# Moving the weight sums between gaps, and the order of three turns on VectorE, in a linear-attention and mixture kernel

## The chip, the cores and the metric

The kernel runs on one core of a Trainium2 chip. The metric is the device time of one execution in microseconds (us), lower being better; for the kernel before it is the median of three runs. All data are 32-bit floats.

## What is computed

Two blocks are chained. The first is a linear recurrence over time (4 batches, 8 heads, 768 steps, head width 40): each head holds a 40 x 40 state.

```
for t in range(S):
    y[t]  = r[t] @ state
    Sa    = state @ a[t]
    state = state * w[t] - outer(Sa, b[t]) + outer(v[t], k[t])
```

Its output is laid out as 3072 tokens of 320 features, `x`. The second block is a mixture of four experts with hidden width 1024:

```
p   = domain_probs / (sum(domain_probs) + 1e-9)
out = sum over e of  p[:, e] * (relu(x @ w1[e]) @ w2[e])
```

## The kernel before

**Units and passes.** The sequence is cut in chunks of 64 steps, and the batches in pairs, so there are 24 units of 64 steps of two batches and all heads. The text counts them from 0: unit 3 is the fourth. Inside a chunk the recurrence becomes small matrix products and a triangular solve. A loop (`for u in range(1, NU)`) makes one pass for each unit. In pass `u` three units are in work at once: unit `u` finishes (its last products with the state and its features `xT`), unit `u+1` has its solve merged and its state products begun, and unit `u+2` goes through `within` and starts its solve. The third pass of the change's title is that of unit 2 and the fifth that of unit 4, if the work ahead of the loop is counted as unit 0's.

**`within` (L402)** prepares a unit. On VectorE it turns W by 32 x 32 blocks (`turn_raw`, L239), scans it to a decay G (L439), takes a reciprocal (L451), makes the tiles `n_tok` (L471) and `k_tok` (L476), turns A (`AT`, L478) and multiplies it by G (L480), and turns V and R (`VT`, `RT`, in `turn_rv`, L421). TensorE then makes the scores `pc` from RT and VT (`causal_scores`, L463), and `pfe` from AT and the turned `n_tok` and `k_tok`. The turns all stand under line 241 in the profile.

**`substitute` (L542)** is the triangular solve of a unit. VectorE and ScalarE copy `blocks` out of `F`, VectorE turns them to `M` (L553) and does two steps (L565, L569), and then GpSimd (POOL in the profile) runs some 48 small operations on `Z` (L580, L593), in a chain. **`merge` (L599)** turns the result back on VectorE (`Qc` L604, `QTc` L606); TensorE makes `pY` from QTc, ScalarE copies `Yq`, TensorE makes `pQ`, ScalarE copies `QT` (L627).

**`step` (L636)** joins a unit to the state: `prn` on TensorE; `RH` on VectorE (L654) and `SN` on ScalarE (L659), both out of `prn`; then `psat` on TensorE, which needs RH and QT; then `pxr`, `pdy`, the state's update and the features.

**The mixture** is work for TensorE that fills the waits of all this. It stands in a list `todo` of pieces: `ups` makes hidden activations (`ph`, relu on ScalarE to `hs`), `down` multiplies them by w2 (`po`, `p`) and VectorE adds the product, scaled by the gate, to the output tile `osb` (L789, L791). The products `ph`, `po`, `p` share three slots of PSUM (tag "mm", `bufs=3`). For the first two units (one chunk) the product with w2 is plain. From the second chunk on, two units are done together by Strassen's scheme with seven products for eight: it needs sums of activations (`add_h`, L897) and **sums of blocks of w2** (`add_weights`, L863): five VectorE operations of 128 x 640 elements for each of four experts, 20 in all, made once. Three of the five are written to a tile `sums`, two over parts of w2 itself, so an expert's sums may come only after its plain products of the first chunk.

**What sets the order.** Each pass has four gaps. `gap(n)` first runs as many weight sums as `sums_at` says for its number `4 * u + n`, then one or two pieces of `todo`. A scheduler at build time lays out each engine's queue; an instruction that is marked with `keep_in_program_order` keeps its place in the program on its engine, the others go where the scheduler finds them ready. [...] All matmuls are marked up to pass 5 (`EARLY`), the weight sums, `Qc`, `QTc`, `blocks`, `M` and the first solve steps always. In `within` the helper `pin` (L406) marks an instruction only for units 0 to 3 (`PADDED` is 3); the turns of V and R are not marked at all.

**In pass 2 to 4** the program runs, in this order: gap 0; the scan's use and `n_tok`, `k_tok` and the turns of unit `u+2`; gap 1; the rest of unit `u`'s step; the products `pc` and `pfe` of unit `u+2`; the merge of unit `u+1` and the solve of unit `u+2`; gap 2; W's turn and the scan of unit `u+3`; `RH` of unit `u+1`; gap 3; `psat` of unit `u+1`.

## Time and profile before

| | |
|---|---|
| median of three runs | 1103.84 us (1103.26 to 1104.54) |
| the profiled execution | 1102.3 us, its span 1100.6 us |
| TensorE busy | 1070.0 us (97% of the span) |
| VectorE busy | 756.6 us (69%) |
| ScalarE busy | 353.0 us (32%) |
| GpSimd busy | 502.9 us (46%) |
| the 20 weight sums on VectorE | 12 of 845 ns and 8 of 872 ns, from 138.2 to 252.5 us |
| granted TensorE clock, mean | 0.991 |

The span is the time between the first and the last recorded instruction; the execution's own time has 1.7 us more around it, and lies 1.5 us under the median of the runs. PE is TensorE's matmuls, PEld its weight loads, DVE is VectorE, ACT ScalarE, POOL GpSimd, and SPq the queue that issues most DMAs. "L863" is line 863 of the kernel. A wait is listed with the instruction that waited and, after the arrow, the one whose end released it, as far as the profile can tell; "issue" means that the profile names no releaser.

### The profile page before, as it was taken

The page shows a single profiled execution, that of the slowest core. Times are in us where ns is not written, and L with a number is a line of the kernel's source. Part 1 is how long each engine was busy: PE and PEld are TensorE (multiplying, and loading weights), DVE is VectorE, ACT ScalarE, POOL GpSimd, SP SyncE. Part 2 cuts the span into 40 slices and gives each one's busy share as a digit, 9 for nine tenths or more (in the row PEclk, how much of TensorE's full clock was granted, in tenths as well). Part 3 has the DMA queues.
Part 4 walks back from the last instruction along what each step waited for, and adds up shares of the span by engine and source line. Part 5 has one row for each costly group of instructions (what it writes and reads, how often), then busy time and mean ns, then how long its engine had stood idle before and what let it go on. Part 6 is the DMA issues. An engine that isn't in the chain of part 4 may idle for free.

```text
span 1100.6 us, 38528 instructions
## 1 busy us (share of the span) xinstructions
PE 1070.0 (97%) x16102; PEld 955.8 (87%) x16102; DVE 756.6 (69%) x1551; ACT 353.0 (32%) x956; POOL 502.9 (46%) x1274
## 2 busy tenths in 40 slices
PE   6799899999999999999999999999999999999998
PEld 6677788789998999898999989989998989988887
DVE  7766668887777776767767768767767677543343
ACT  2432444223233233243233242332332432321110
POOL 5106677753463653743734635636537437430000
PEclk9799999999999999999999999999999999999999
DMA  7776545425345363354353444443552532222320
GB/s 117 226 247 138 136 103 117 119 55 136 98 111 127 98 140 97 94 146 103 93 144 94 102 121 104 116 120 84 127 123 65 147 85 67 98 69 82 104 76 13
DMA packets 268868, 122.18 MB, mean 111 GB/s; under 512 B 213736, under 2 KB 242072, under 8 KB 268696
## 3 DMA queue, kind: packets, MB, share of 16 engines
q1 hardware_dynamic: 265416, 119.12, 43.0%
q8 instruction: 127, 2.08, 0.8%
q10 hardware_dynamic: 3280, 0.61, 0.3%
q14 instruction: 45, 0.37, 0.1%
HBM read 111.79 MB, written 3.93 MB: 105 GB/s over the span
## 4 chain that ended last, share of the span: by engine, by line
PE 81%; DVE 7%; POOL 5%; ACT 3%; issue 2%; DMA 1%; SPq 0%; ACTq 0%; DVEq 0%; POOLq 0%
PE ph L76 35%; PE p L76 28%; POOL Z L593 3%; PE pdy L76 3%; PE psat L76 2%; PE pxr L76 2%; POOL Z L580 2%; PE prn L76 1%; PE pfe L76 1%; PE pQ L76 1%; PE po L76 1%; PE pc L76 1%; DVE Z L590 1%; PE pY L76 1%; DVE M L553 1%
## 5 line engine op out<-in xcount | busy, mean ns | idle before, releaser
L76 PE MATMUL ph<-xT,w1p 128*128 128x256 f32 (+3 forms) x3040 | 446.3, 377 | 4.0 <-issue 3.9
L76 PEld LDWEIGHTS ph<-xT,w1p 64*64 64x64 f32 (+1 forms) x3040 | 338.5, 162 | 72.7 <-issue 29.0
L593 POOL TENSOR_TENSOR Z<-Z 128x31 f32<-128x31 f32 (+7 forms) x704 | 260.0, 369 | 55.2
L897 DVE TENSOR_TENSOR a<-hs 128x512 f32<-128x512 f32 x220 | 151.8, 707 | 104.7 <-ACT hs L778 104.7
L580 POOL TENSOR_TENSOR Z<-M,Z 128x62 f32<-128x62 f32 (+7 forms) x352 | 144.1, 409 | 132.3 <-DVE M L569 106.4
L778 ACT ACTIVATE hs<-ph 128x512 f32<-128x512 f32 (+1 forms) x208 | 115.3, 564 | 226.5 <-PE ph L76 225.4
L76 PE MATMUL p<-sums,a 128*128 128x160 f32 x1056 | 164.9, 299 | 0.0
L76 PEld LDWEIGHTS p<-sums,a 128*128 128x128 f32 x1056 | 152.8, 190 | 2.2
L791 DVE SCALAR_TENSOR_TENSOR osb<-p,gate,osb 128x320 f32<-128x320 f32 (+1 forms) x243 | 108.1, 481 | 57.8 <-PE p L76 53.6
L550 POOL COPY below<-F 32x256 f32<-32x256 f32 x48 | 22.8, 475 | 198.7 <-ACT F L506 197.0
L76 PE MATMUL p<-w,a 128*128 128x160 f32 x704 | 105.9, 301 | 0.2 <-ACT hs L778 0.2
L76 PE MATMUL p<-w,hs 128*128 128x160 f32 x704 | 102.9, 299 | 0.0
L76 PEld LDWEIGHTS p<-w,hs 128*128 128x128 f32 x704 | 100.2, 190 | 2.2
L76 PEld LDWEIGHTS p<-w,a 128*128 128x128 f32 x704 | 98.3, 190 | 3.0 <-ACT hs L778 3.0
L612 POOL COPY QT<-QTc 32x256 f32<-32x256 f32 x96 | 51.7, 539 | 76.9 <-DVE QTc L606 67.7
L553 DVE STREAM_TRANSPOSE M<-blocks 128x1024 f32<-128x1024 f32 x24 | 47.4, 1977 | 38.1 <-ACT blocks L547 37.9
L700 ACT COPY RS<-pxr 64x256 f32<-64x256 f32 x88 | 32.2, 366 | 105.2 <-DVE SX L400 43.1
L451 DVE RECIPROCAL gp<-gp 128x320 f32<-128x320 f32 x24 | 51.6, 2151 | 0.7
L535 ACT COPY EV<-pev 64x160 f32<-64x160 f32 x96 | 23.1, 286 | 89.7 <-PE pev L76 89.3
L604 DVE STREAM_TRANSPOSE Qc<-Z 128x256 f32<-128x256 f32 x24 | 15.0, 627 | 46.2 <-POOL Z L593 46.1
L627 ACT COPY QT<-pQ 32x128 f32<-32x128 f32 x96 | 24.6, 256 | 59.9 <-PE pQ L76 58.2
L659 ACT COPY SN<-prn 128x256 f32<-128x256 f32 x44 | 14.9, 372 | 78.6 <-DVE RH L654 78.6
(149 smaller groups left out, 1357.5 us busy)
## 6 DMA issues: line engine op xcount, KB each, us to landing
w1p<-in_moe_w_dram SPq DMA_DIRECT2D x95, 512.0 KB
w1p<-in_moe_w_dram SPq DMA_DIRECT2D x190, 64.0 KB
w<-in_moe_w_dram SPq DMA_DIRECT2D x4, 1280.0 KB
sums<-in_moe_w_dram SPq DMA_DIRECT2D x9, 512.0 KB
natW<-in_w_dram SPq DMA_DIRECT2D x48, 80.0 KB
natB<-in_b_dram SPq DMA_DIRECT2D x48, 80.0 KB
natK<-in_k_dram SPq DMA_DIRECT2D x48, 80.0 KB
out_dram<-osb SPq DMA_DIRECT2D x46, 80.0 KB
```

Source lines behind the costliest of these rows:

```text
L76: return stated(nc.tensor.matmul(**k))
L451: pin(nc.vector.reciprocal(out=gp[:], in_=gp[:]))
L535: nc.scalar.copy(out=of_slot(q.EV[half(p)], i ^ p)[:, :, 0:D], in_=pev[i][half(p)])
L553: ins = nc.vector.transpose(out=M[:], in_=cols)
L580: ins = eng.tensor_tensor(out=Z[:, 1:3, 0:n, j + 1:Q], in0=M[:, j:j + 2, None, j + 1:Q].to_broadcast([P, 2, n, m]), in1=Z[:, here, 0:n, j: ...
L593: eng.tensor_tensor(out=z[:, 0], in0=z[:, 0], in1=z[:, x], op=ALU.add)
L612: ins = nc.gpsimd.tensor_copy(out=q.QT[quarter(i), :, quarter(i % 2)], in_=QTc[quarter(i)])
L627: nc.scalar.copy(out=of_slot(to[quarter(2 * r)], y), in_=src)
L700: nc.scalar.copy(out=RS[half(s), x ^ s::2], in_=prs[x][half(s)].rearrange("p (j i) t -> p j i t", i=2),)
L778: nc.scalar.activation(out=h[:, i * HF // 2:(i + 1) * HF // 2, 0:n], in_=ph[i][:], func=ACTF.Relu,)
L791: nc.vector.scalar_tensor_tensor(out=to, in0=p, scalar=sc, in1=to, op0=ALU.mult, op1=ALU.add)
L897: nc.vector.tensor_tensor(out=t[:], in0=x, in1=y, op=op)
```

## The change

Three edits. The turns of V and R are handed to `pin`, so that for unit 3 they keep their place in the program. For units 3 to 6 `turn_rv()` is called ahead of A's turn and of the multiplication of A by G, and no longer after them; from unit 7 on the order stays. The table `sums_at` is replaced: the same 20 sums in the same order are spread over gaps 9 to 17 where they were spread over gaps 9 to 22.

| gap number | 9 | 10 | 11 | 12 | 13 | 14 | 15 | 16 | 17 | 18 | 19 | 20 | 21 | 22 |
|---|---|---|---|---|---|---|---|---|---|---|---|---|---|---|
| before | 1 | 1 | 1 | 1 | 1 | 1 | 1 | 1 | 1 | 1 | 2 | 3 | 2 | 3 |
| after | 3 | 2 | 1 | 2 | 1 | 4 | 2 | 2 | 3 | | | | | |

Gaps 9 to 11 belong to pass 2, 12 to 15 to pass 3, 16 to 19 to pass 4, 20 to 22 to pass 5.

```diff
                 if q.u >= PADDED:
-                    turn_raw(t[:], n["raw" + x][:])
+                    pin(turn_raw(t[:], n["raw" + x][:]))
                     continue
...
         pin(other.tensor_tensor(out=q.K[:, :, 0:D], in0=n["K"][:], in1=gp[:], op=ALU.mult))
+        if PADDED <= q.u < EARLY + 2:
+            VT = turn_rv()
         if q.u > 1:
             pin(turn_raw(q.AT[:], n["rawA"][:]))
...
-        if q.u >= PADDED:
+        if q.u >= EARLY + 2:
             VT = turn_rv()
         yield
...
-    sums_at = {4 * 2 + n: 1 for n in range(1, 11)}
-    sums_at.update({4 * 4 + 3: 2, 4 * 5 + 0: 3, 4 * 5 + 1: 2, 4 * 5 + 2: 3})
+    sums_at = dict(zip(range(4 * 2 + 1, 4 * 4 + 2), (3, 2, 1, 2, 1, 4, 2, 2, 3)))
```

## The prediction

> **What bounds the kernel now.** I read the page's busy rows and slices first, then a table by stages of 25 us, then what TensorE (PE) waited for, and last the order on VectorE (DVE) around each wait.

> ```profile
> PE 1070.0 (97%) x16102; PEld 955.8 (87%) x16102; DVE 756.6 (69%) x1551; ACT 353.0 (32%) x956; POOL 502.9 (46%) x1274
> ```
> ```profile
> 100.00:125.00 25.00, 21.01 (x481) 17.90 (x480) 16.56 (x33) 11.27 (x35) 16.23 (x48) 1.00 0.70 165
> 125.00:150.00 25.00, 23.88 (x409) 20.29 (x409) 18.57 (x37) 8.28 (x24) 17.86 (x47) 1.00 0.52 102
> ...
> 200.00:225.00 25.00, 22.35 (x441) 19.06 (x443) 19.69 (x40) 8.82 (x26) 17.99 (x41) 0.93 0.53 119
> 225.00:250.00 25.00, 24.06 (x350) 21.35 (x341) 22.11 (x45) 6.76 (x17) 12.95 (x27) 1.00 0.19 50
> 250.00:275.00 25.00, 25.00 (x355) 22.87 (x354) 17.35 (x33) 10.37 (x28) 8.09 (x23) 1.00 0.60 146
> ```
> The first number after the stage's length is TensorE's busy time. From 250 us on TensorE has no idle time, so nothing that VectorE saves there can shorten the run. All that this change can win lies in TensorE's holes between 100 and 250 us:

> ```profile
> PE ph L76 <- issue: 3.4, 2, 2.1
> PE pc L76 <- DVE RT L241: 3.1, 3, 1.8
> PE pQ L76 <- ACT Yq L627: 1.3, 1, 1.3
> ```
> Three numbers stand at each wait: the sum, how often, the longest. The second is three scores `pc` that wait for the turn of R: 1.78 us at 104.97 (unit 3), 0.37 at 138.37 (unit 4), 0.94 at 246.33 (unit 7). The `pQ` wait is at 114.48. The first, "issue", is a hole of 1.32 us at 124.30 and one of 2.09 at 207.47. The last is in truth a wait: in the trace TensorE's sequencer sits in a semaphore wait from 204.59 to 209.50, and VectorE's semaphore rises at 209.47, the end of the second of these:

> ```profile
> 207.45 0.50 DVE L791 SCALAR_TENSOR_TENSOR osb<-p,gate,osb 128x320 f32<-128x320 f32 x1
> 207.90 0.67 DVE L897 TENSOR_TENSOR a<-hs 128x512 f32<-128x512 f32 x1
> ...
> 208.49 0.68 DVE L565 TENSOR_TENSOR Z<-M 128x512 f32<-128x512 f32 x1
> 209.09 0.37 DVE L791 SCALAR_TENSOR_TENSOR osb<-p,minus_gate,osb 128x160 f32<-128x160 f32 x1
> ```
> The two adds empty `p75`, and the second half of the next `ph` needs its PSUM slot. VectorE is late there. The hole also halves the clock: the granted clock is 0.5 for 3.41 us from about 210, which costs 3.41 / 2 = 1.7 more. This place costs 3.8 us in all.

> [...] the solve's first product takes 0.29 us at 118.65 and 0.74 at 146.32, beside a weight sum. [...] the sums have 845 and 872, and in a row they come each 0.85 us (1.69 for two at 218.02). I use 0.85. [...]

> **V and R ahead of A.** Per unit the same four instructions of 0.70, 0.69, 0.70 and 0.67 us change places; nothing is added, and no DMA is issued in the moved step. For unit 3 the marks fix the new order:

> ```profile
> 102.27 0.70 DVE L241 STREAM_TRANSPOSE AT<-rawA 128x512 f32<-128x512 f32 x1
> 103.00 0.69 DVE L480 TENSOR_TENSOR AT<-AT,G 128x512 f32<-128x512 f32 x1
> 103.61 0.70 DVE L241 STREAM_TRANSPOSE VT<-rawV 128x512 f32<-128x512 f32 x1
> 104.24 0.67 DVE L241 STREAM_TRANSPOSE RT<-rawR 128x512 f32<-128x512 f32 x1
> ```
> RT ends at 104.91; now V starts at 102.27 and RT ends two operations (0.73 + 0.61 = 1.34) earlier, at 103.57. R's loads are issued by 99.79 and their landing is hidden already. `pc` starts 1.3 us earlier. Behind the moved A are `pfe` (110.59) and SP's next load of `rawA` (issued at 105.86): A's product ends at 104.9, so neither waits. Next late is `pY`, which needs QTc (ends 111.33, set by the solve on GpSimd): TensorE arrives at 110.3 and now waits 1.1 us there. But `F` can be copied 1.3 earlier, so ScalarE's copies of F and `blocks` (111.85 to 113.34) no longer stand ahead of Yq: pY ends about 112.0, Yq takes 1.06, and `pQ` starts near 113.25 for 114.48. **Gain 1.2 us**; lower bound 0.2 if ScalarE's order changes, upper 1.3. Units 4 to 6 are not marked: A was turned at 119.08, 150.20 and 181.26, long before V (135.73, 156.84, 189.02), because its data come sooner; I expect no change. Only unit 4's 0.37 could be won, and 0.7 lost if A is pushed behind V: I take 0.

> **Sums taken out of gaps 18 to 22.** Eleven times 0.85 is 9.4 us of VectorE. They lie at 209.98, 218.02, 226.01, 247.12 and 250.18. The first is after the add that frees PSUM; VectorE then idles 1.55, 0.85, 1.83 and 2.23 us before 230.89, so the delay is absorbed; at 247 to 252 TensorE does not wait. The hole at 246.33 comes of VectorE's unbroken run from 230.89, with no sum in it. **Gain 0**; it could be up to 0.9 if the shorter queue changes R's place.

> **Sums put into gaps 9 to 17.** The extra ones are 2, 1, 0, 1, 0, 3, 1, 1 and 2.

> Pass 2 (gaps 9, 10): VectorE runs without a pause from 130.93 to 151.6, so three extra sums (2.55 less 0.1 of idle) move RH from an end at 149.54 to 152.0. `psat` starts at 151.89: **loss 0.2**. If ScalarE keeps SN (which waits for RH) ahead of the last QT copies, QT ends at 150.96 + 2.45 = 153.4 and the loss is 1.5. Gap 12's extra sum falls in idle time (4.77 us before 162.31).

> GpSimd: M of unit 4 comes 1.65 later (gap 9). What a sum costs GpSimd is not shown alone; the solves give a bound: 20.8 us for unit 3 (118.65 to 139.4, one sum at its end), 23.0 for unit 4 with four sums, so about 0.57 each. Two more in unit 4's solve are 1.1, and it ends at 169.37 + 2.8 = 172.2, less the loss above, where VectorE reaches its turn Qc at 170.73. Unit 5's M is so 0.7 to 1.3 later.

> Pass 3 (gap 14): four sums stand marked behind unit 5's M and ahead of RH:

> ```profile
> 176.70 0.69 DVE L569 TENSOR_TENSOR M<-M,Z 128x512 f32<-128x512 f32 x1
> 177.31 0.82 DVE L863 TENSOR_TENSOR sums<-w 128x640 f32<-128x640 f32 x1
> ...
> 180.06 0.54 DVE L654 TENSOR_TENSOR RH<-prn,EV 128x160 f32<-128x160 f32 x2
> ```
> RH ends at 180.60, `psat` starts at 182.34: 1.74 us of cover. Three sums are 2.55, and Qc's wait adds 0.7 to 1.3: 1.5 to 2.1 too late. If the scheduler lets the sum of activations at 179.33 pass behind RH it is 0.3 to 0.8; if ScalarE again keeps SN ahead of QT (QT ends at 182.03, cover 0.3), 3.5. I take **loss 2.0**.

> Pass 4 (gap 17): two extra sums, 1.7, come at 197.93; VectorE has 0.17 + 0.21 + 0.70 = 1.1 of idle before Qc at 202.98, so the adds that free `p75` end 0.6 later. If the solve of unit 5 is late (start 0.7 later, seven more sums 4.0, less the 2.0 that TensorE has lost), it is 205.7 instead of 202.95 and they end 2.7 later. Between these I take **loss 2.0**. Gaps 15 and 16 are covered by 1.46 and 1.72 us of idle at 187.6 and 190.

> **Sum**: -1.2 + 0.2 + 2.0 + 2.0 = +3.0 us. The profiled execution (1102.3, span 1100.6 and 1.7 around it) becomes 1105.3. It lies 1.5 below the median of its runs, so the same step on the median 1103.84 gives 1106.8.

> **Rivals.** (a) *Faster.* One mechanism: in VectorE's queue the adds of `p75` fall ahead of M, since a VectorE that is later finds `p75` done sooner. From an end before 206.9 on (2.6 earlier) the hole at 207.47 and its half clock are gone, 3.8 us. With the other terms: -1.2 + 0.2 + 2.0 - 3.8 = -2.8, 1101.0. For it: the first add already slipped in behind M (207.45), where the queue had a pause. Against: M and the steps after it stand earlier in the program. (b) *Nothing measurable.* The scheduler puts RH ahead or the solve is less late: losses 0.1, 0.8 and 0.6 against 1.2, 1104.1. For it: the pauses at 152, 155 and 187. Against: no pause from 162.98 to 182.8 but 0.3. (c) *Much slower.* ScalarE's order stays as it is: 1.5 + 3.5 + 2.7 - 1.2 = +6.5, 1110.3. For it: this order (SN, a QT, SN, three QT) stands in both passes. Against: with RH late the scheduler would find QT ready first. (d) That the new order does nothing for unit 3 can't be, as it is marked.

> **How the numbers follow.** Forecast 1106.8: 0.40. (c) 0.18; (b) 0.18; (a) 0.24. 0.2% is 2.2 us, about what a measurement of this kernel can tell from no change. So faster 0.24, same 0.18, slower 0.58. Both signs are likely: the forecast's own range, with pass 3 between 0.8 and 2.1 and pass 4 between 0.6 and 2.7, is 1104.4 to 1107.8. The wide range goes down into (a) (1100.0, half of unit 7's 0.9 won as well) and up to (c) with a little over it, 1111.0.

> **What would show it.** RT of unit 3 ends near 103.6, `pc` right after, `pQ` near 113.2. `psat` of unit 4 shows a hole of some 2 us ahead of it, behind RH; the hole at 207 is wider. From 250 on TensorE's busy time is full as before. The prediction is wrong if the hole at 207 is gone, or if RH ends before TensorE comes to `psat` in passes 2 and 3.

## The result and the profile after

The changed kernel takes 1106.87 us (median; 1103.58 to 1110.61). The kernel before, run beside it on the same chip, takes 1103.20. The ratio is **1.0031, 95% interval 1.0021 to 1.0042**: slower by some 3.4 us. The profiled execution took 1106.6 us, with a span of 1104.9 (before: 1102.3 and 1100.6).

In the changed file the lines behind L476 stand two lower: sums L865, osb L793, RH L656, Qc L606. First the busy row and the table by stages of 25 us of the kernel after (columns: TensorE's matmuls, its weight loads, VectorE, ScalarE, GpSimd; then the granted clock, the DMA share and GB/s):

```profile
PE 1071.7 (97%) x16102; PEld 956.8 (87%) x16102; DVE 758.1 (69%) x1551; ACT 353.2 (32%) x956; POOL 506.5 (46%) x1274
```
```profile
100.00:125.00 25.00, 21.24 (x481) 18.01 (x480) 16.36 (x33) 11.79 (x36) 16.20 (x48) 1.00 0.69 164
125.00:150.00 25.00, 23.51 (x406) 19.83 (x406) 20.21 (x36) 7.28 (x19) 18.24 (x45) 1.00 0.51 104
...
175.00:200.00 25.00, 22.56 (x416) 19.26 (x415) 23.80 (x42) 10.19 (x31) 20.04 (x34) 0.93 0.39 108
200.00:225.00 25.00, 23.56 (x348) 20.05 (x350) 20.45 (x40) 7.49 (x20) 17.05 (x43) 1.00 0.46 110
225.00:250.00 25.00, 23.64 (x432) 21.39 (x425) 18.38 (x41) 8.22 (x21) 12.23 (x31) 1.00 0.24 62
250.00:275.00 25.00, 25.00 (x400) 22.46 (x391) 15.02 (x30) 10.17 (x29) 7.31 (x22) 1.00 0.56 139
```

GpSimd is busy 3.6 us longer with the same 1274 instructions. The clock of 0.93 stood in the stage from 200 us and now stands in the one from 175. The waits of TensorE between 80 and 262 us (sum, how often, longest):

```profile
PE ph L76 <- issue: 2.9, 2, 1.6
PE pc L76 <- DVE RT L241: 2.4, 3, 1.1
PE pxr L76 <- issue: 1.9, 1, 1.9
...
PE pNT L79 <- DVE n_tok L471: 0.7, 1, 0.7
PE pQ L76 <- ACT Yq L629: 0.6, 1, 0.6
...
PE psat L76 <- DVE gl L443: 0.4, 1, 0.4
```

New are `pNT`, `psat` and, with no releaser, `pxr`. (The profile names `gl` at `psat`; `gl` is a small operation of VectorE between the two halves of RH, and it is RH that `psat` reads.) I compared the starts of the same matmuls in both traces; the offsets, after less before, show where time is lost and won back:

| TensorE's mark (time before) | offset, us | what lies since the mark above |
|---|---|---|
| pc, unit 3 (104.97) | -0.61 | V and R ahead of A |
| pg (130.81) | -0.33 | hole at 124: 1.60 for 1.32 |
| pc, unit 4 (138.37) | +0.73 | pNT waits 0.70 for n_tok |
| psat, unit 4 (182.34) | +1.20 | psat waits 0.35 behind RH |
| pg, unit 6 (191.33) | +5.24 | hole of 1.94 at 187, then half clock |
| pY, unit 5 (215.87) | +2.82 | hole at p75: 1.31 for 2.09, no half clock after it |
| end (1100.59) | +4.30 | small waits over passes 5 to 23 |

The turns of unit 3 (VectorE) stand in the new order, but RT waits for its data:

```profile
102.13 0.69 DVE L241 STREAM_TRANSPOSE VT<-rawV 128x512 f32<-128x512 f32 x1
103.59 0.71 DVE L241 STREAM_TRANSPOSE RT<-rawR 128x512 f32<-128x512 f32 x1 [0.77 <-DMA rawR<-in_r_dram]
104.23 0.67 DVE L241 STREAM_TRANSPOSE AT<-rawA 128x512 f32<-128x512 f32 x1
```

In pass 2 the three sums of gap 9 run ahead of Y, which started at 130.93 before, and n_tok follows:

```profile
128.63 2.86 DVE L865 TENSOR_TENSOR sums<-w 128x640 f32<-128x640 f32 x3 [5.32 <-PE ph L76]
131.41 0.74 DVE L717 TENSOR_TENSOR Y<-pdy,RS 128x256 f32<-128x256 f32 x2
...
136.99 0.44 DVE L471 SCALAR_TENSOR_TENSOR n_tok<-natB,gp 128x320 f32<-128x320 f32 x1
```

In pass 3 the four sums of gap 14 stand ahead of RH, as foreseen; `psat` is 1.2 us late:

```profile
177.47 0.69 DVE L571 TENSOR_TENSOR M<-M,Z 128x512 f32<-128x512 f32 x1
178.08 0.82 DVE L865 TENSOR_TENSOR w<-w 128x640 f32<-128x640 f32 x1
178.81 2.49 DVE L865 TENSOR_TENSOR sums<-w 128x640 f32<-128x640 f32 x3
...
183.10 0.29 DVE L656 TENSOR_TENSOR RH<-prn,EV 128x160 f32<-128x160 f32 x1
183.32 0.15 DVE L443 TENSOR_TENSOR gl<-gl,G 128x8 f32<-128x8 f32 x1
183.40 0.31 DVE L656 TENSOR_TENSOR RH<-prn,EV 128x160 f32<-128x160 f32 x1
```

What follows on TensorE wasn't foreseen (last bracket: idle time ahead of the row):

```profile
183.54 1.06 PE L76 MATMUL psat<-QT,RH 64*64 64x64 f32 x30 [0.35 <-DVE gl L443]
...
186.25 0.69 PE L76 MATMUL pxr<-RT,SaT 64*64 64x64 f32 x30
188.88 0.27 PE L76 MATMUL pxr<-RT,SaT 64*64 64x64 f32 x1 [1.94 <-issue]
```

The hole stands in the middle of a run of equal matmuls, with no semaphore wait on TensorE in the trace there. After it the clock is halved for 3.41 us (the next 16 `ph` take 5.29 us for 3.72). And in pass 4, on VectorE, first before, then after:

```profile
202.98 0.63 DVE L604 STREAM_TRANSPOSE Qc<-Z 128x256 f32<-128x256 f32 x1 [0.70 <-POOL Z L593]
```
```profile
206.74 0.78 DVE L400 COPY_PREDICATED VC<-mask_up,pc 128x256 f32<-128x256 int32 x2 [0.21 <-PE pc L76]
207.41 0.62 DVE L606 STREAM_TRANSPOSE Qc<-Z 128x256 f32<-128x256 f32 x1
...
211.89 0.53 DVE L793 SCALAR_TENSOR_TENSOR osb<-p,gate,osb 128x320 f32<-128x320 f32 x1
...
213.53 0.40 DVE L793 SCALAR_TENSOR_TENSOR osb<-p,minus_gate,osb 128x160 f32<-128x160 f32 x1
```

Before, Qc waited for the end of GpSimd's solve; after, it stands right behind VC, the copy of the scores `pc`. The last add ends at 213.93 (before: 209.46), and TensorE goes on at 214.03.

### The profile page after: what moved, and what is told of

Read it like the earlier page. It is cut to its first block, busy times and chain, and to the rows that moved or that the text cites. A ratio compares the mean times of both kernels' runs of the same rounds, so it can differ in the third digit from the quotient of the medians.

```text
span 1104.9 us, 38525 instructions
## 1 busy us (share of the span) xinstructions
PE 1071.7 (97%) x16102; PEld 956.8 (87%) x16102; DVE 758.1 (69%) x1551; ACT 353.2 (32%) x956; POOL 506.5 (46%) x1274
## 3 DMA queue, kind: packets, MB, share of 16 engines
q8 instruction: 127, 2.08, 0.8%
## 4 chain that ended last, share of the span: by engine, by line
PE 75%; DVE 10%; POOL 7%; issue 3%; ACT 3%; SPq 1%; DMA 1%; DVEq 0%; POOLq 0%; ACTq 0%
PE ph L76 32%; PE p L76 26%; POOL Z L595 4%; POOL Z L582 2%; PE pdy L76 2%; PE psat L76 2%; PE pxr L76 2%; DVE M L555 1%; PE pQ L76 1%; PE prn L76 1%; PE po L76 1%; PE pfe L76 1%; PE pc L76 1%; DVE Z L592 1%; ACT Yq L629 1%
## 5 line engine op out<-in xcount | busy, mean ns | idle before, releaser
L76 PE MATMUL ph<-xT,w1p 128*128 128x256 f32 (+3 forms) x3040 | 445.9, 377 | 3.6 <-issue 3.4
L76 PEld LDWEIGHTS ph<-xT,w1p 64*64 64x64 f32 (+1 forms) x3040 | 338.7, 162 | 71.7 <-issue 28.7
L595 POOL TENSOR_TENSOR Z<-Z 128x31 f32<-128x31 f32 (+7 forms) x704 | 263.7, 375 | 55.2
L899 DVE TENSOR_TENSOR a<-hs 128x512 f32<-128x512 f32 x220 | 152.0, 708 | 115.4 <-ACT hs L780 115.4
L76 PE MATMUL p<-sums,a 128*128 128x160 f32 x1056 | 164.9, 299 | 0.0
L76 PEld LDWEIGHTS p<-sums,a 128*128 128x128 f32 x1056 | 152.8, 190 | 2.2
L793 DVE SCALAR_TENSOR_TENSOR osb<-p,gate,osb 128x320 f32<-128x320 f32 (+1 forms) x243 | 108.1, 481 | 59.0 <-PE p L76 55.2
L76 PE MATMUL p<-w,a 128*128 128x160 f32 x704 | 106.4, 301 | 1.3 <-ACT hs L780 1.1
L76 PE MATMUL p<-w,hs 128*128 128x160 f32 x704 | 102.9, 299 | 0.0
L76 PEld LDWEIGHTS p<-w,a 128*128 128x128 f32 x704 | 98.4, 190 | 4.5 <-ACT hs L780 4.5
L76 PEld LDWEIGHTS p<-w,hs 128*128 128x128 f32 x704 | 100.2, 190 | 2.2
L606 DVE STREAM_TRANSPOSE Qc<-Z 128x256 f32<-128x256 f32 x24 | 15.1, 629 | 47.0 <-POOL Z L595 46.8
```

The costliest lines, as they stand in the source:

```text
L76: return stated(nc.tensor.matmul(**k))
L595: eng.tensor_tensor(out=z[:, 0], in0=z[:, 0], in1=z[:, x], op=ALU.add)
L793: nc.vector.scalar_tensor_tensor(out=to, in0=p, scalar=sc, in1=to, op0=ALU.mult, op1=ALU.add)
L899: nc.vector.tensor_tensor(out=t[:], in0=x, in1=y, op=op)
```

## The experiments

Each was timed against the kernel before in the same session on the same chip. e1 to e4, e5 to e8 and e9 to e11 are three sessions on three chips, so across these groups only the ratios are compared.

### The two halves of the change

`e1_turns` has the new turns and the old table; `e2_sums` the new table and the old turns.

> The turns of V and R ahead of A, with the weight sums left as before. Theory: only unit 3's order changes, and pc of unit 3 and pQ come 0.6 us earlier, so 0.5 us faster than before (ratio 0.9995), with the hole behind p75 near 207 us as before. Rival (the turns are what costs: A's later product or R's loads delay something): 1 to 4 us slower, with a new wait on AT or RT in passes 1 to 4.

> The new table of weight sums, with the turns left as before. Theory: the sums make all of the loss, so 3.5 to 4.5 us slower than before (ratio 1.003 to 1.004): 0.7 us of wait at pNT of unit 4, 0.8 at psat of unit 4, and an unexplained hole of 2 us behind it. Rival (turns cost): within 1 us of before.

Measured: e1 **0.9985** (0.9974 to 0.9996), e2 **1.0046** (1.0032 to 1.0060). The two add up: -0.15% + 0.46% = +0.31%, the ratio of the whole change. e2's waits were not all where they were expected: `pNT` does not wait, `psat` waits 0.37, the hole behind it is 1.31 without a half clock, and the loss comes at `p75` instead, 2.55 with a half clock. e1 won more than expected, since RT doesn't wait in it:

```profile
102.36 0.69 DVE L241 STREAM_TRANSPOSE VT<-rawV 128x512 f32<-128x512 f32 x1
102.99 0.66 DVE L241 STREAM_TRANSPOSE RT<-rawR 128x512 f32<-128x512 f32 x1
103.58 0.66 DVE L241 STREAM_TRANSPOSE AT<-rawA 128x512 f32<-128x512 f32 x1
```

`pc` comes 1.31 us earlier against the start of its pass and `pQ` 1.25: the step predicted at 1.2. In the ten profiles with the new turns of unit 3 the gain of `pc` is 1.31 to 1.36 in eight, and 0.63 and 0.50 in two (the changed kernel and e11); in these two RT waits for R's data. Their last load of R was issued 5.6 and 5.7 us after the pass began, in the eight others after 3.6 to 4.7. All of the loss comes from the table.

### What the hole without a wait is

The 1.94 us hole at 187, and the one at 124 that the prediction left as "issue", stand at the same kind of place. Count TensorE's entries in the trace (matmuls, weight loads, semaphore instructions): the holes begin at entries 3521 and 5825 or 5826, 256 x 13 + 193 and 256 x 22 + 193 (or 194). The page's list of DMA queues shows what comes at that rate:

```profile
q8 instruction: 127, 2.08, 0.8%
```

127 packets, 2.08 MB: 16,384 bytes each in the traces of before and after, where TensorE has 32,606 entries, so one packet for 256.7 entries. The page calls the queue's kind "instruction", and I take its packets for the fetch of TensorE's instructions. The ends fit too: at 187 (after) the packet's start is at 186.36 and its end at 187.24, and TensorE goes on at 188.88, 1.64 us later; at 124 it goes on 1.40 us (before) and 1.46 us (after) behind the end of the packet that starts at 123.10 and 122.89. A block is here the 256 entries up to the next such place. The block before entry 5825 begins in the middle of `psat`'s stage, and 512 KB of weights for w1p are issued close by (times of the trace; the fetch is the next packet of q8):

| kernel | block begins | w1p issued ahead of it by | next fetch starts, us after the block | hole at 187 |
|---|---|---|---|---|
| before | 182.58 | 0.14 | 0.53 | none |
| e5 (below) | 185.01 | 0.13 | 0.53 | 0.19 |
| after | 184.16 | 0.94 | 2.20 | 1.94 |
| e10 (below) | 185.31 | 0.94 | 2.20 | 1.97 |
| e6 (below) | 182.98 | 1.60 | 2.06 | 1.68 |

The wait of `psat` lies between the issue of the load and the block. With it, the load's data move ahead of the fetch (up to 200 KB in half a microsecond: 418 and 381 GB/s in two slices of 0.25 us of after), and in the three late cases the fetch starts when 540 to 640 KB have passed. To see whether the hole follows the count or the place in the program, two kernels got 16 more warm-up matmuls at the start, which shifts the later entries:

```diff
-    keep_warm(16)
+    keep_warm(20)
...
-    keep_warm(10)
+    keep_warm(14)
...
-    keep_warm(12)
+    keep_warm(20)
```

> The changed kernel with 16 more warm-up matmuls in the idle time of the first 20 us, so that each block of 256 TensorE instructions begins 64 instructions earlier in the program. Theory: the hole of 1.9 us at 186.9 is a late instruction fetch, which stood behind a load of w1p; with the block's start moved it goes, and with it the half clock behind it: 3 us faster than the changed kernel, within 1 us of before. Rival (the hole is a wait for data or PSUM): the hole stays where it is, 3.4 us slower than before.

> The kernel before with the same 16 more warm-up matmuls. Theory: the hole of 1.3 us at 124.3 is a late fetch as well and goes, so 0.5 to 1.3 us faster than before, and the wait behind p75 near 207 stays. Rival (warm-ups cost time at the start, holes stay): 0 to 1.5 us slower.

Measured: e3 (changed kernel) 1.0068 (1.0047 to 1.0088), e4 (kernel before) 1.0026 (1.0015 to 1.0036). The times miss: the warm-ups weren't free. By 70 us TensorE is 3.5 us late in e3 and 2.5 in e4 (part of it can be the varying start, see the end). The holes answer the question: in both, the one at 124 is still at entry 3521, though the program moved by 64 entries, so that it now falls into `pxr` where it was in `ph` (2.29 and 2.64 us long); in e3 the one at 187 is gone, with `psat`'s wait (0.37) still there. The hole belongs to the entry, and of all that the profile shows the packets of q8 recur with the entries. That a late packet makes the hole, and that the weights' load is what delays it, is read from these times; no run moved either by itself. And e3 is no faster for losing the hole at 187: its hole at `p75` is 3.64 us, with a half clock.

### Taking the sums away from single waits

My theory A was now that the loss sits at single places: `pNT` behind gap 9's three sums, `psat` behind gap 14's four, and the hole that follows. Rival B: the amount of sums moved into passes 2 to 4 costs, wherever they stand. Four tables, all with the new turns (gaps 9 to 22):

```diff
-  after      3 2 1 2 1 4 2 2 3
+  e5_gap14   3 2 1 4 2 0 2 3 3
+  e6_gap9    1 2 2 3 1 4 2 2 3
+  e7_spread  0 1 1 2 2 0 2 2 2 2 2 2 2
+  e8_late    0 0 0 0 0 0 0 0 0 4 4 4 4 4
```

> The changed kernel with one thing different: none of the weight sums in gap 14 (they go to gaps 12, 13 and 16), so RH of unit 4's tile is no longer behind four sums. Theory A (the changed kernel loses at single places: n_tok behind gap 9's sums 0.7, psat of unit 4 behind gap 14's sums 0.4 to 1.2, and what follows from that: the late instruction fetch at 187 of 1.9 and its half clock 1.6): the wait ahead of psat at 183 goes, and so does the hole at 187 with its half clock; ratio to the kernel before 1.000 (0.999 to 1.001), some 3 us under the changed kernel's 1.003. Rival B (the loss is the amount of VectorE and GpSimd work moved into passes 2 to 4, wherever it stands): 1.003 as for the changed kernel. Rival C (the fetch is late with or without the sums, as it depends on the 512 KB load, which moves along): the psat wait goes, the hole at 187 stays: 1.002.

> The changed kernel with one thing different: one weight sum in gap 9 in place of three, the other two in gaps 11 and 12. Theory A: the 0.70 us wait of pNT for n_tok at 137 goes, the psat wait at 183 and the hole at 187 stay since four sums still stand ahead of RH: 0.7 us under the changed kernel, ratio to the kernel before 1.0025. Rival B (amount of work moved, wherever it stands): 1.003, as two sums only move 20 us. If the psat wait goes too, since TensorE comes 0.7 earlier to it but GpSimd's solve ends up to 1.1 earlier, 1.001 or less is possible.

> The turn edit of the change with another table of weight sums: none in gaps 9 and 14, one or two in every other gap from 10 to 21. Theory A: no wait at n_tok or psat, the turn's gain of 1.2 is kept: ratio 0.998 (0.997 to 0.9995), as the turn edit with the old table (0.9985) or a little better. Rival B (amount of work moved into passes 2 to 4: twelve sums here, nine in the kernel before, twenty in the changed one): 0.9995 to 1.0005. Rival D (sums in gaps 17 to 21 are not free: they delay the adds that empty p75 at 207 or R's turn of unit 7 at 246): 1.001.

> The turn edit of the change with all twenty weight sums in gaps 18 to 22, four in each, and none in passes 2 to 4. Theory A and the prediction's step that sums in gaps 18 to 22 cost nothing while VectorE idles there: 0.998 (0.997 to 0.9995), the best that a table can do for passes 2 to 4. Rival D: 17 us of sums between 210 and 252, where the profile of before leaves VectorE 6.5 us idle up to 231 and none from there to 246, put R's turn for unit 7 (0.94 late already) up to 8 us late: 1.003 to 1.007, and the hole stands ahead of pc at 246.

Measured: e5 **1.0041** (1.0025 to 1.0056), e6 1.0025 (1.0014 to 1.0037), e7 1.0015 (1.0003 to 1.0026), e8 1.0107 (1.0090 to 1.0124).

e6 came as A said: no wait at `pNT`, the others stay. But **e5 breaks A** and is near what B said. Its `psat` doesn't wait and the hole at 187 has shrunk to 0.19, yet nothing is won: the hole at `p75` is now 4.06 us, with a half clock after it (smaller losses stay too: `pNT` waits 0.39, and `psat` of pass 2 is stretched by some 0.8, as QT stands behind SN on ScalarE). TensorE reached that place sooner and waited longer there. Its VectorE:

```profile
207.72 0.62 DVE L606 STREAM_TRANSPOSE Qc<-Z 128x256 f32<-128x256 f32 x1 [2.72 <-POOL Z L595]
208.38 0.45 DVE L608 STREAM_TRANSPOSE QTc<-Qc 128x256 f32<-128x256 f32 x1
...
212.13 0.53 DVE L793 SCALAR_TENSOR_TENSOR osb<-p,gate,osb 128x320 f32<-128x320 f32 x1
...
213.76 0.40 DVE L793 SCALAR_TENSOR_TENSOR osb<-p,minus_gate,osb 128x160 f32<-128x160 f32 x1
```

VectorE stands idle 2.72 us for the end of GpSimd's solve. The add that empties `p75` ends 6.4 us after Qc starts (6.5 in before and after). e7 speaks against A as well: it has no wait at `pNT` or `psat` and no hole at 187, A gave it 0.998, and it lost at `p75`, where the hole is 3.16 us and the half clock lasts 6.83.

e8 shows the limit on the other side. With all sums late, some products come ahead of their sums in the program and read other weights, so part of the output is other values; only its waits are read. TensorE waits 8.3 us for `sums` at 204 and 4.7 us for `w` at 250. Rival D had the sign right and the place wrong: the sums have due times.

### The solve beside the sums

In each trace I took unit 5's solve on GpSimd, the sums that VectorE starts in it, and Qc's start (an operation can start some 0.1 us before the record of the one ahead ends):

| kernel | sums in the solve | the solve, us | its end | VC's end | Qc starts | released by |
|---|---|---|---|---|---|---|
| before | 3 | 25.4 | 202.95 | 202.28 | 202.98 | solve |
| e7 | 6 | 26.3 | 203.34 | 201.56 | 203.38 | solve |
| e5 | 8 | 27.0 | 207.68 | 205.00 | 207.72 | solve |
| e6 | 10 | 28.4 | 205.56 | 204.44 | 205.59 | solve |
| after | 10 | 28.3 | 206.60 | 207.51 | 207.41 | VC |

Each sum costs the solve 0.4 to 0.8 us: (28.3 - 25.4) / 7 = 0.41 between before and after, (28.3 - 23.05) / 10 = 0.52 against the run without a sum below, and (25.4 - 23.05) / 3 = 0.78 for the three of before against that run. The sums are not all that differs beside the solve. The first product of a solve shows the same: in the kernel before it takes 0.29 us at 89.54 and 118.65 with no sum beside it, and 0.74 at 146.32, 177.54 and 210.21 beside one. Why it takes longer there, no run shows. So theory G: **two chains** meet at Qc. One is GpSimd's solve, the other TensorE's own way to `pc`, whose copy VC stands ahead of Qc in VectorE's queue. In the changed kernel both are late, TensorE's by 0.9 more. Taking away either alone should win little. Three tables test it:

```diff
-  e1_turns       1 1 1 1 1 1 1 1 1 1 2 3 2 3
+  e9_none_late5  1 1 1 1 1 0 0 0 0 5 2 3 2 3
+  e10_no15to17   3 2 1 2 1 4 0 0 0 1 1 1 2 2
+  e11_best       1 2 1 2 2 0 0 0 0 2 2 3 2 3
```

> The turn edit of the change, the old table of weight sums, but the four sums of gaps 14 to 17 (beside GpSimd's solve for unit 5) put into gap 18, which has five. Theory G, formed from the traces so far: the end of that solve sets when p75 is emptied (the hole at 207 to 214 ends 6.6 us after the solve in every trace), and each sum made beside a solve lengthens it by 0.45 us (25.4 us with four sums, 26.5 with six, 27.2 with eight, 28.4 to 28.5 with eleven). So the solve takes 23.6 us, p75 is free 1.8 us earlier than in the turn edit alone, and the half clock after the hole has a smaller chance: ratio to the kernel before 0.9970 (0.9955 to 0.9980). Rival A (only the waits of pNT and psat count): no change against the turn edit alone, 0.9985. Rival D (five sums in gap 18 delay the next adds that empty p75 by 3.4 us, a new hole near 214): 0.9990 to 1.0005.

> The changed kernel with the seven weight sums of gaps 15 to 17 moved to gaps 18 to 22; gap 14 keeps its four sums ahead of RH, gap 9 its three. Theory G: two chains run side by side in passes 3 and 4 of the changed kernel. TensorE's own (psat wait, late instruction fetch at 187, half clock) brings it to p75 at 212.7, and GpSimd's solve with eleven sums empties p75 at 214.0. Here the solve has four sums: 3.1 us shorter, p75 empty near 210.9, TensorE comes at 212.7 and does not wait; its own losses stay. Ratio to the kernel before 1.0018 (1.0010 to 1.0025), 1.3 us under the changed kernel. Rival A (the loss is the waits behind the sums of gaps 9 and 14 alone): 1.003, no change. Rival B (amount of sums anywhere in passes 2 to 4): 1.001.

> The turn edit of the change with eight weight sums in gaps 9 to 13 (1, 2, 1, 2, 2), none in gaps 14 to 17, and 2, 2, 3, 2, 3 in gaps 18 to 22. Theory G: unit 5's solve has no sum beside it and takes 23.6 us; unit 4's has seven in place of four, 1.4 us longer, which is about what Qc of unit 4 leaves (1.4): start of unit 5's solve 0 to 0.5 later. Ratio to the kernel before 0.9970 (0.9955 to 0.9985), the best version so far. Rival B (amount of sums in passes 2 to 4: eight here, nine in the kernel before): 0.9985. Rival D is weaker than in the run with five sums in gap 18: two there delay the next adds by 0.85 us.

Measured: e9 **0.9974** (0.9965 to 0.9984), e10 1.0022 (1.0012 to 1.0033), e11 0.9982 (0.9971 to 0.9993). The solve takes 23.05 us in e9 and 23.08 in e11, with no sum beside it, and 24.5 in e10 with three.

e5 took away `psat`'s wait and the hole at 187 and kept eight sums in the solve: 1.0041. e10 took seven sums from the solve and kept TensorE's holes: 1.0022, whose interval overlaps with the changed kernel's. e9 did both, with one sum in gap 9: 0.9974. That fits two parallel chains. So does the stretch from `pg` of pass 2 (130.81 before) to `pY` of unit 5, which leaves out the start of the program:

| kernel | the stretch, us | hole at 187 | hole at `p75` | half clock in it |
|---|---|---|---|---|
| before | 85.06 | none | 2.09 | once |
| e4, table of before | 83.15 | none | 2.10 | none |
| e1, table of before | 83.23 | 0.23 | 1.47 | none |
| after | 88.21 | 1.94 | 1.31 | once |
| e2, table of after | 88.94 | 1.31 | 2.55 | once |
| e3, table of after | 88.35 | none | 3.64 | once |
| e5 | 89.21 | 0.19 | 4.06 | once |
| e6 | 87.42 | 1.68 | 2.54 | none |
| e7 | 87.57 | none | 3.16 | once, twice as long |
| e10 | 86.42 | 1.97 | 1.29 | none |
| e9 | 82.86 | none | 1.30 | none |
| e11 | 83.04 | none | 1.29 | none |

With the new table (after, e2, e3) the stretch takes 88.2 to 88.9 us, with the hole at 187 or without it: there the late fetch only moves the loss to another place. Where the solve is short it costs: 86.42 in e10 for 82.86 in e9 (which has fewer sums in gaps 9 and 14 as well).

The times alone don't rule out rival B. Count the sums ahead of gap 18: 5 in e9, 8 in e11, 9 in e1, 12 in e7, 13 in e10 and 20 in after, e5 and e6. The ratios rise in this order, and e11 came nearer to B's 0.9985 than to G's 0.9970. What speaks for G is what released Qc in each trace. One part of G's expectation failed: in e10 the hole at `p75` was to go, and it stays at 1.29 us. It is 1.29 to 1.31 in after, e9, e10 and e11, all four with Qc behind VC: the way from TensorE's `pc` through VC, Qc and the adds back to `p75` is itself 1.3 us too long. So the hole does not end 6.6 us after the solve "in every trace", as e9's expectation has it (7.4 in after). And in e9 only 0.8 of the 2.09 us was won there, and 1.6 with the half clock that didn't come (against TensorE's time at pass 4's start, 2.4 us are gained by `pY`). Five sums in gap 18 cost no visible wait; GpSimd's next product beside them takes 3.68 us:

```profile
209.85 3.68 POOL L582 TENSOR_TENSOR Z<-M,Z 128x62 f32<-128x62 f32 x1 [2.92 <-DVE M L571]
213.61 0.94 POOL L595 TENSOR_TENSOR Z<-Z 128x31 f32<-128x31 f32 x2
```

With no sum beside it this product takes 0.29 us in e5 (at 214.91); the one of e9's own solve of unit 5, which has none either, takes 1.22 (at 178.14). Unit 6's solve has time to spare.

**e9 beats both kernels.** A further gain over e1 isn't shown: the intervals overlap (0.9965 to 0.9984, 0.9974 to 0.9996), and e1's profile, too, has only 1.47 us of hole at `p75` and no half clock there, which makes e9 shorter by 0.4 us over the stretch above.

## Why the prediction came out as it did

The direction and the total were right: +3.0 us was worked out, some 3.4 were measured. The terms behind the sum were not all right, and their errors cancel: that the total came so close is in part luck. (Two sums are off in the prediction itself. Its own range adds up to 1104.2 to 1107.6, not 1104.4 to 1107.8, and the low end with half of unit 7's wait is 1100.6, not 1100.0.)

- **V and R ahead of A, -1.2: right in mechanism and in size**, where R's data are there (1.31 in e1). In the profile of after it was 0.6. The sentence that failed is "their landing is hidden already": RT starts earlier now, R's loads were issued later in that execution, and RT waits 0.77 us for them. Units 4 to 6 kept their order, as predicted.
- **Pass 2, +0.2: wrong place and too small.** This is the first term that failed. RH wasn't late at `psat`. ScalarE kept its old order here (SN, a QT, SN, three QT), against the assumption, but QT ended at 152.51, just ahead of `psat` at 152.63. Two of the three sums of gap 9 fell into idle time of VectorE, so M of unit 4 came 0.7 later and not 1.65. The three sums of gap 9 went ahead of Y (131.41 for 130.93) and n_tok came late: `pNT` waits 0.70, offset +1.06 from `pg` to `pc`. I had counted only what stands ahead of RH. With one sum there (e6) the wait is gone.
- **Pass 3, +2.0: the cause right, the size wrong in both directions.** ScalarE took QT first here, as assumed. `psat` lost 0.76, 0.35 of it ahead of its first matmul and the rest by its second half. But behind it came what is read above as a late instruction fetch, with 1.94 of hole and 1.57 of half clock; with smaller waits that makes 4.5. The prediction saw the hole at 124, called it "issue" and left it unexplained; the same thing came at 187.
- **Pass 4, +2.0: wrong sign in the offset.** The sums of gap 17 didn't stand at 197.93; they were taken ahead of V's turn (191 to 195). The solve was late, 206.60 where the bad branch said 205.7, but it did not set the pace: TensorE was 5.24 late when it got there, so that VC came later still. The hole, which was to be wider, shrank from 2.09 to 1.31, and its half clock didn't recur: -2.42. e3 shows what the prediction pictured: without the hole at 187, Qc waits 1.69 us for the solve, and the hole at `p75` is 3.64.
- **Gaps 18 to 22, 0: right** as far as the traces show: e9 makes fifteen sums there at no visible wait. That sums do better there than beside the solve of unit 5 is suggested by e9 against e1 and not shown, as their intervals overlap.
- **Rivals.** (a) needed `p75` to be emptied earlier: it was emptied 4.5 us later. (c), ScalarE's old order with RH late, came in pass 2 and cost nothing there; in pass 3 it didn't come.
- The further 1.5 us from `pY` of unit 5 to the end aren't explained by the change: all the other profiles lose there too (e8 aside), 0.2 to 3.0 (e4, with the table and the turns of before, 0.9), against a profiled execution of before that lay under its median. Why that execution had fewer late waits stays open.

## What to carry to other kernels

Work on VectorE that is "in idle time" isn't free while GpSimd runs a chain that ends on the path: count it in that chain (here 0.4 to 0.8 us for each sum of 0.85), and place it where the chain has time. When two chains meet at one buffer, undo both before judging either: with TensorE's alone shortened the hole at `p75` only grew (e5: 4.06 us for 1.31), with the solve's alone it stayed (e10: 1.29). The holes of TensorE in the middle of equal matmuls, with no semaphore, lay 2304 entries apart here (9 x 256) or one more, and went with a late packet of the queue "instruction", 2.06 us and more after its block. The one at 187 came and went with delays of about one microsecond elsewhere (0.14 or 0.94 us from the load's issue to the block), so look whether the loss goes with it or only moves.
